# Attention with beacon keys, then an MLP: the first batch's scores by pairs of heads, and its first MLP products in two parts

## The chip, the cores and the metric

The kernel runs on one core of a Trainium2 chip. The metric is the device time of one execution in microseconds. Three runs of the kernel before took 323.22, 322.51 and 323.13 us: median 323.13 us.

## The reference

Batch 8, heads 8, 576 tokens of 64 elements, 16 beacon keys ahead of the 576 keys. The attention's output is laid out as 4608 tokens of 512 elements and goes through an MLP with 2048 hidden columns.

```
k_all, v_all = concatenate([beacon, own], axis=2)          # 592 keys
scores = q @ k_all.T / 8 ; token t sees all beacons and keys 0..t
a = softmax(scores) ; attn = a @ v_all                     # 8 x 8 x 576 x 64
x = attn as [4608, 512]
h = x @ w_in ; g = h * sigmoid(1.702 h) ; out = g @ w_out  # 512 -> 2048 -> 512
```

## The kernel before, in words

**Sets.** Four heads of one batch are a *set*; there are 16 (sets 0 and 1 are batch 0, sets 2 and 3 batch 1, and so on). A head's 64 elements lie as 32 partitions times 2, so the four heads of a set fill 128 partitions. q and k of a set (`qn`, `kn`) are loaded by one DMA each (L417) and turned by VectorE into `qT` and `kT` (L473; the beacon keys by a small one, L466). The values of a batch come in six loads: the beacons' (L422) and five blocks of keys, called V0 to V4 here (L426, L433).

**Scores and exponentials.** A set's causal scores are 1664 columns of a head, cut into *chunks*. For each chunk TensorE multiplies kT by qT head by head, each head in its own 32 rows of the array (`e_qk`, L506), and ScalarE takes the exponential into `E` (`e_exp`, L517). For batch 0, columns 0 to 511 of a set belong to the first half of its tokens (288), the other 1152 columns to the second half, in three chunks of 384. Diagonal blocks are masked, on VectorE with a `keep` tile (L531) for the first half of sets 0 and 1, else on GpSimd (L538); the `keep` tiles are made on GpSimd (L333, L334).

**Banks.** Of the 8 PSUM banks, four hold the tile `s`, one chunk's scores of four heads. The other four (`u0` to `u3`) are a ring for all other products; a bank opens again when the last reader of what it held (norm, z1, gate, evacuation) is done. In this kernel chunks 1 and 2 do not go to `s` but take all four ring banks, one a head, with four exponentials of one head each (`RINGED`); chunk 0 is read in two exponentials (`SPLIT`).

**Values and norms.** For a set and a half of its tokens there are three products of E (`e_av`, L597), for batches 0 and 1: one with `ones` for the sums (called x=2), one each for the even and odd elements of V. VectorE turns the sums into reciprocals (`z1` L607; `z2` L613 and L618) and the norm (L631) writes the result to `xT`.

**MLP.** Tokens are taken in groups: 0 to 255, 256 to 511, then 512 each. Of group 0 a *first product* `m1.0.n` makes two blocks of 128 hidden columns in one ring bank: 8 matmuls (`e_m1`, L655), over four slices of d_model, of which the first two come from set 0 and the last two from set 1. Then tanh on ScalarE (L669), the gate on VectorE (L688, which frees the bank), the second product (L700). Later groups use another gelu and a Strassen-like scheme (L769, L856). `w_in` comes in eight loads (L439): columns 0-511, 512-1023, 1024-1535 and 1536-2047 (a, b, c, d here), each in two halves of d_model (0 and 1); `w_out` in four loads (L446).

**Order.** Nothing is scheduled by the hardware or a search at build time: `op()` declares operations, numbered in order of declaration, with an engine, what they need and which ring bank they take, and the table `ORDER` lists by these numbers the order of every engine. `Plan.run` only goes through these lists; the planner's durations decide which ring bank a tile takes and how warm-up matmuls fill TensorE's first 20 us (L1377). Loads are issued by GpSimd, at most eight in flight: GpSimd waits at the ninth until the one eight earlier has landed, and all behind it in its order waits too, masks included.

The order of the first operations, decoded from `ORDER` (qk = a chunk's scores, av S.x.h = product x of set S and half h, m1.G.n and m2.G.t = first and second MLP products, turn S = transposition; VectorE's casts and memsets left out):

```
PE   qk0 qk3 qk1 qk4 qk2 qk5 av0.2.0 av1.2.0 av1.1.0 qk6 av0.0.0 av0.2.1 av0.1.0 av1.0.0 qk7
     m1.0.0 m1.0.2 m1.0.4 m1.0.6 av0.0.1 av0.1.1 av1.2.1 av1.1.1 av1.0.1 m1.0.8 m1.0.10 m1.0.14
     m1.0.12 m1.1.0 qk8 m1.1.4 m1.1.2 m1.1.12 qk9 ...
DVE  turn0q turn0k turn1k turn1q mask0 mask0 mask1 mask1 mask0 mask1 z1.0 z2.0 z1.1 z2.1 norm0 norm0
     norm1 norm1 z1.0 turn2q z2.0 gate gate gate norm0 norm0 z1.1 z2.1 norm1 gate norm1 gate turn2k ...
POOL q0 k0 k1 q1 V0 b1 a0 V4 a1 beaconV V2 V1 c1 keep b0 mask0 q2 k3 V3 c0 mask0 k2 d0 mask0 d1 mask1 q3 ...
```

(In this kernel qk0, 2, 3 and 4 are set 0's chunks in the order first half, then the three of 384; qk1, 5, 6 and 7 are set 1's.)

Of the kernel before, what the change touches and what calls it, by code (L numbers as in the profile page):

```python
# [8 lines left out]
F32 = mybir.dt.float32  # L9
AFT = mybir.ActivationFunctionType  # L10
# [51 lines left out]
    ],  # L62
    "DVE": [
# [23 lines left out]
    "POOL": [  # L87
# [8 lines left out]
    ],  # L96
# [6 lines left out]
    ],  # L103
# [4 lines left out]
    ],  # L108
}


# [133 lines left out]
def kernel(  # L245
# [13 lines left out]
    B, H, S, D = q.shape  # L259
# [1154 lines left out]
```

## Time and profile before

| what | value |
|---|---|
| median of three runs | 323.13 us |
| the profiled execution itself | 323.13 us |
| its span in the trace | 321.4 us, 10238 instructions |
| TensorE busy | 310.9 us, 97% |
| VectorE, ScalarE, GpSimd busy | 245.7, 219.9, 112.7 us |
| granted TensorE clock, 0 to 300 us | 1.00 |
| loads and stores, mean | 90 GB/s over the span |

The profile shares the span into 40 slices of 8 us and gives each engine's busy share in each in tenths, and the mean busy share of the DMA engines. The chain of waits follows the end of the program back through whatever released each piece of work. The timeline lists an engine's instructions in order, merged where alike: start, length, line, tiles, shape, count, and in brackets the idle time ahead of them with what ended it. Busy time of matmuls overlaps, so the start of the next entry tells how long one occupies TensorE, not its length.

### The profile page before, as it was taken

Reading aid. Unit: us, or ns where it says so; the run is one execution under the profiler, and the core shown is the slowest. Engines: PE = TensorE matmul, PEld = TensorE weight load, DVE = VectorE, ACT = ScalarE, POOL = GpSimd, SP = SyncE. Lnnn points to the kernel's source line nnn. Section 1 sums busy time; section 2 is a strip of 40 time slices with the busy share of each in tenths; the row PEclk is TensorE's granted clock in tenths of the full one; section 3 lists DMA queues with packets and bytes.
Section 4 is the critical chain, followed back from the end, with each engine's and each line's share of the span. In section 5 each row is a group of like instructions: output and inputs, shape, how many; then the busy total and the mean of one; then the engine's idle time right before and its main releaser. Section 6 shows DMA issues by size and latency. Waiting matters only on the chain.

```text
span 321.4 us, 10238 instructions
## 1 busy us (share of the span) xinstructions
PE 310.9 (97%) x4465; PEld 230.0 (72%) x4465; DVE 245.7 (76%) x481; ACT 219.9 (68%) x277; POOL 112.7 (35%) x178
## 2 busy tenths in 40 slices
PE   7779999999999999999999999999999999999995
PEld 6557765644886467754778878746888888888884
DVE  3579963997894888976888969888988975684683
ACT  1783778686767787598867685778779786665520
POOL 7777558590226703573083208320320000000000
PEclk9999999999999999999999999999999999999999
DMA  7999999998028961299174707700021000010113
GB/s 120 159 194 206 195 198 179 197 188 104 2 63 115 168 91 35 20 163 122 23 78 88 120 4 71 107 33 2 4 72 61 2 20 17 33 68 34 68 58 107
DMA packets 58222, 28.85 MB, mean 90 GB/s; under 512 B 41280, under 2 KB 53568, under 8 KB 58176
## 3 DMA queue, kind: packets, MB, share of 16 engines
q0 software_dynamic: 47552, 18.49, 49.4%
q1 hardware_dynamic: 10560, 9.69, 9.2%
q8 instruction: 35, 0.57, 0.7%
q14 instruction: 11, 0.09, 0.1%
q10 hardware_dynamic: 64, 0.01, 0.0%
HBM read 37.22 MB, written 9.44 MB: 145 GB/s over the span
## 4 chain that ended last, share of the span: by engine, by line
PE 91%; DMA 3%; POOL 3%; ACT 1%; issue 1%; DVE 0%; POOLq 0%
PE u L769 31%; PE u L655 26%; PE u L856 11%; PE u L597 10%; PE s L506 8%; PE u L700 5%; DMA w<-in_moe_w_in_dram 3%; POOL w L439 1%; ACT E L517 1%; POOL vb L433 1%; POOL kn L417 0%; ACT L676 0%; POOL qn L417 0%; POOL E L538 0%; DVE xT L631 0%
## 5 line engine op out<-in xcount | busy, mean ns | idle before, releaser
L517 ACT ACTIVATE E<-s 128x2048 f16<-128x2048 f32 (+5 forms) x63 | 95.6, 1532 | 41.4 <-PE s L506 37.7
L655 PE MATMUL u<-xT,w 128*128 128x256 f16 (+1 forms) x512 | 87.4, 326 | 0.7 <-issue 0.5
L538 POOL TENSOR_SCALAR_AFFINE_SELECT E<-E 128x512 f16<-128x512 f16 (+3 forms) x78 | 48.1, 634 | 91.4 <-ACT E L517 91.3
L655 PEld LDWEIGHTS <-w 128*128 128x128 f16 x512 | 49.3, 98 | 33.7 <-issue 2.1
L676 ACT ACTIVATE g<-u 128x512 f16<-128x512 f32 x80 | 43.4, 600 | 15.7 <-PE u L655 15.2
L769 PEld LDWEIGHTS <-g 128*128 128x128 f16 x512 | 48.4, 98 | 6.9
L785 DVE SCALAR_TENSOR_TENSOR osb<-u,osb 128x512 f32<-128x512 f32 x48 | 32.9, 685 | 22.8 <-PE u L769 18.2
L769 PE MATMUL u<-w,g 128*128 128x256 f16 x384 | 50.2, 273 | 0.0
L769 PEld LDWEIGHTS <-sA 128*128 128x128 f16 x384 | 36.6, 98 | 4.9
L506 PEld LDWEIGHTS <-kT 32*128 32x128 f16 x1376 | 24.6, 92 | 19.7 <-issue 12.8
L884 ACT ACTIVATE g<-u 128x512 f16<-128x512 f32 x48 | 27.0, 602 | 15.0 <-PE u L856 9.1
L506 PE MATMUL s<-qT,kT 32*128 32x32 f16 (+20 forms) x1328 | 33.1, 228 | 2.4 <-ACT E L517 1.9
L769 PE MATMUL u<-tB,sA 128*128 128x256 f16 x256 | 34.2, 273 | 0.0
L631 DVE TENSOR_TENSOR xT<-u,rz 128x352 f16<-128x352 f32 (+2 forms) x52 | 26.1, 519 | 6.1 <-PE u L597 5.3
L433 POOL DMA_DIRECT2D vb<-in_v_dram x32 | 27.5, 861 | 3.8 <-DMA qn<-in_q_dram 1.5
L597 PE MATMUL u<-E,vb 128*32 128x352 f16 (+8 forms) x928 | 27.3, 262 | 0.7 <-DMA vb<-in_v_dram 0.4
L597 PEld LDWEIGHTS <-vb 128*32 128x32 f16 (+1 forms) x928 | 20.0, 96 | 6.1 <-issue 2.1
L556 DVE TENSOR_TENSOR zs<-zs,E 128x1344 f16<-128x1344 f16 (+2 forms) x36 | 21.6, 601 | 1.1
L473 DVE STREAM_TRANSPOSE qT<-qn 128x576 f32<-128x576 f32 x16 | 19.8, 1235 | 3.2 <-DMA qn<-in_q_dram 2.4
L473 DVE STREAM_TRANSPOSE kT<-kn 128x576 f32<-128x576 f32 x16 | 20.1, 1257 | 0.9 <-DMA kn<-in_k_dram 0.3
L856 PEld LDWEIGHTS <-w 128*128 128x128 f16 x192 | 18.7, 98 | 2.2
L856 PE MATMUL u<-xT,w 128*128 128x256 f16 x144 | 20.1, 273 | 0.0
(76 smaller groups left out, 388.2 us busy)
## 6 DMA issues: line engine op xcount, KB each, us to landing
out_dram<-osb SPq DMA_DIRECT2D x36, 256.0 KB, 2.3
qn<-in_q_dram POOLq DMA_DIRECT2D x16, 288.0 KB, 6.4
kn<-in_k_dram POOLq DMA_DIRECT2D x16, 288.0 KB, 6.2
vb<-in_v_dram POOLq DMA_DIRECT2D x24, 128.0 KB, 5.5
w<-in_moe_w_in_dram POOLq DMA_DIRECT2D x8, 256.0 KB, 9.4
w<-in_moe_w_out_dram POOLq DMA_DIRECT2D x4, 512.0 KB, 11.1
vb<-in_v_dram POOLq DMA_DIRECT2D x8, 112.0 KB, 5.9
vb<-in_v_dram POOLq DMA_DIRECT2D x8, 80.0 KB, 6.6
```

The source lines that it names most:

```text
L433: nc.gpsimd.dma_start(out=t[0 : hi - lo, j, h0:h1, :], in_=v[b, h0:h1, lo:hi, :].rearrange("h n d -> n h d"),)
L473: nc.vector.transpose(out=f32(dst.rearrange("p n e -> p (n e)")).rearrange("p (r t) -> p t r", t=TR), in_=f32(src[:, :]).rearrange("p (t c ...
L506: nc.tensor.matmul(ss[i][h][:, o : o + w], kT[s % NB2][r : r + 32, j * P : (j + 1) * P, d], qT[s % NB2][r : r + 32, a : a + w, d], start=( ...
L517: nc.scalar.activation(out=Es[s][:, :, c0:c1] if h is None else Es[s][:, h, c0:c1], in_=sall[i][:, :, o : o + c1 - c0] if h is None else s ...
L538: nc.gpsimd.affine_select(out=blk, in_=blk, compare_op=ALU.is_ge, fill=0.0, base=off + (Nb if j == 0 else 0), pattern=[[0, Q], [1, w]], ch ...
L597: nc.tensor.matmul(u[32 * h : 32 * h + 32, a:e], lhs, src[0:kw, h, col : col + e - a], start=first, stop=last, skip_group_check=s >= EARLY ...
L655: nc.tensor.matmul(u[:, o + a - t0 : o + e - t0], w1t[:, kp, nt * P : (nt + 1) * P], xT[:, kp, a % XR : (e - 1) % XR + 1], start=(kp == 0) ...
L676: nc.scalar.activation(out=gts[g][:, n0:n1, 0:w], in_=rings[("m1", g, n0)][:, 0 : n * w].rearrange("p (n w) -> p n w", n=n), func=AFT.Gelu ...
L769: nc.tensor.matmul(u[:, HM * mt : HM * (mt + 1)], lhs[:, n, mt * P : (mt + 1) * P], rhs[:, n, :], start=(n == 0 and mt == 0 and p not in ( ...
L785: nc.vector.scalar_tensor_tensor(out=osbs[(g, dst)][:, :], in0=rings[("p", g, p)][:, :], scalar=scale_of(g), in1=osbs[(g, src)][:, :], op0 ...
L856: nc.tensor.matmul(u[:, HM * n : HM * (n + 1)], lhs[x][:, (2 * i + n) * P : (2 * i + n + 1) * P], rhs[:, x, :], start=fresh and n == 0 and ...
L884: nc.scalar.activation(out=gts[g][:, n : n + 2, HM * h : HM * (h + 1)], in_=rings[src][:, :].rearrange("p (n w) -> p n w", n=2), func=AFT. ...
```

## The change

Batch 0's chunks 0 to 5 get score tiles of their own in place of the ring: two tiles `p0` and `p1` of two banks, for heads 0 and 1 and for heads 2 and 3, which lie where `s` lies later. Chunk 0 ("F") has its scores in one go and two exponentials, one a pair; chunks 1 to 5 ("S") have scores and exponentials by pair, and a pair's scores wait only for the same pair's exponential of the chunk before. Chunks 6 and 7 use `s` as before. The chunks of batch 0 come in another order (set 0 first half; set 0; set 1 first half; set 0, set 1, set 0, set 1, set 1), and the first is not split by columns any more. The first products `m1.0.0` and `m1.0.2` are declared in two parts of two slices of d_model, each needing only one set's norms and one half of W1. `ORDER` is new for all engines; decoded in the same way:

```
PE   qk0 qk1 qk1 qk2 qk2 av0.2.0 av0.0.0 qk3 qk3 av0.1.0 qk4 av1.2.0 qk4 av1.0.0 av1.1.0 qk5 qk5
     m1.0.0(first) m1.0.0(second) m1.0.2(first) qk6 m1.0.6 av0.2.1 qk7 m1.0.4 m1.0.2(second) qk8
     av0.1.1 av0.0.1 av1.2.1 m1.0.8 qk9 m1.0.10 m1.0.12 qk10 av1.0.1 av1.1.1 m1.0.14 qk11 m1.1.0 ...
DVE  turn0q turn0k turn1q turn1k mask0 mask0 mask0 z1.0 z2.0 mask1 mask1 mask1 norm0 norm0 z1.1 z2.1
     norm1 norm1 gate turn2q z1.0 turn2k z2.0 gate gate norm0 z1.1 z2.1 gate norm0 gate gate ...
POOL q0 k0 beaconV q1 k1 V1 V2 V0 V3 b1 a1 a0 keep b0 q2 V4 k2 c1 mask0 c0 d1 d0 q3 mask0 mask0 mask1 k3 ...
```

From about the 95th operation of TensorE, the 47th of ScalarE, the 88th of VectorE and the 79th of GpSimd on, the order is that of before; SyncE's is unchanged.

```diff
+    EARLY1 = (0, 2)
-    SPLIT = True
...
-        CHUNKS += [[(s, 0, HF), (s, HF, EHALF)] if SPLIT and s < 1 else [(s, 0, EHALF)]] + [[(s, EHALF + cut * i, EHALF + cut * (i + 1))] for i in range(3)]
-    CHUNKS[: 4 * HS] = sorted(CHUNKS[: 4 * HS], key=lambda ch: ch[0][1] > 0)
+        CHUNKS += [[(s, 0, EHALF)]] + [[(s, EHALF + cut * i, EHALF + cut * (i + 1))] for i in range(3)]
+    CHUNKS[: 4 * HS] = [CHUNKS[x] for x in (0, 1, 4, 2, 5, 3, 6, 7)]
...
-    RINGED = (1, 2)
+    PAIRED = "FSSSSS"
...
-    def e_qk(i):
-        if i in RINGED:
-            ss[i] = [ring_tile(("qk", i, h)) for h in range(Q)]
+    def e_qk(i, p):
+        heads = {}
+        if i < len(PAIRED):
+            for p in range(2) if p is None else (p,):
+                sc = upper_pool("psp").tile([P, 2, 512], F32, tag=f"p{p}", name=f"p{p}")
+                sall[(i, p)] = sc
+                heads.update({2 * p + x: sc[:, x, :] for x in range(2)})
...
-                for h in range(Q):
+                for h, u in heads.items():
...
+        h0, h1 = (0, Q) if p is None else (2 * p, 2 * p + 2)
         nc.scalar.activation(
+            out=Es[s][:, h0:h1, c0:c1], in_=sall[(i, p)][:, :, o : o + c1 - c0], func=AFT.Exp, scale=0.125,
         )
...
-    def e_m1(g, n0, n1):
+    def e_m1(g, n0, n1, k0=0, k1=NKT):
...
-                for kp in range(NKT if a < e else 0):
+                for kp in range(k0, k1 if a < e else k0):
...
-                        start=(kp == 0),
+                        start=(kp == 0 and (k1 == NKT or nt == n0)) and k0 == 0,
                         stop=(kp == NKT - 1),
+                        skip_group_check=k1 - k0 < NKT,
...
+        halved = i < len(PAIRED)
+        split = halved and PAIRED[i] == "S"
+        for p in range(2) if halved else (None,):
+            if p is None or p == 0 or split:
+                y = p if split else None
+                before = [x for (j, n, z), x in exps.items() if j == i - 1 and y in (None, z)]
+                qks[i] = op(
+                    "PE", w, deps + before + ([qks[i]] if p else []), lambda y=y: e_qk(i, y), kind="qk", pr=0,
...
+            if g == 0 and n0 in EARLY1:
+                plan.partial.add(key)
+                pe, k = None, NKT // HS
+                for hs in range(HS):
+                    pe = op(
+                        "PE", k * n * (w / 2.4 + 2.8),
+                        [norms[(hs, 0, x)] for x in range(2)] + [w1_of[n0][hs], pe],
+                        lambda n0=n0, n1=n1, hs=hs: e_m1(g, n0, n1, k * hs, k * hs + k),
```

More of the change, by code (lines that the diff above doesn't have):

```diff
@@ L162, in run @@
         free = {e: 0 for e in todo}
-        free.update(POOL=900, SP=700)
+        free.update(POOL=1300, SP=700)
         mode, table, order = "m", "e", []
@@ L490, in qk_pieces @@
         return got
-    def e_qk(i):
-        if i in RINGED:
-            ss[i] = [ring_tile(("qk", i, h)) for h in range(Q)]
+    def e_qk(i, p):
[5 more added lines that the diff above has]
+                heads.update({2 * p + x: sc[:, x, :] for x in range(2)})
         else:
             sc = upper_pool(f"pss{plan.late_of(i)}").tile([P, Q, 512], F32, tag="s", name="s")
-            ss[i] = [sc[:, h, :] for h in range(Q)]
-            sall[i] = sc
+            sall[(i, p)] = sc
+            heads = {h: sc[:, h, :] for h in range(Q)}
         for (s, c0, c1) in CHUNKS[i]:
@@ L503, in e_qk @@
             for d in range(2):
-                for h in range(Q):
+                for h, u in heads.items():
                     r = 32 * h
                     nc.tensor.matmul(
-                        ss[i][h][:, o : o + w],
+                        u[:, o : o + w],
                         kT[s % NB2][r : r + 32, j * P : (j + 1) * P, d],
@@ L512, in e_qk, with e_exp @@
                     )
-    def e_exp(i, n, h=None):
+    def e_exp(i, n, p):
         s, c0, c1 = CHUNKS[i][n]
         o = sum(x[2] - x[1] for x in CHUNKS[i][:n])
+        h0, h1 = (0, Q) if p is None else (2 * p, 2 * p + 2)
         nc.scalar.activation(
-            out=Es[s][:, :, c0:c1] if h is None else Es[s][:, h, c0:c1],
-            in_=sall[i][:, :, o : o + c1 - c0] if h is None else ss[i][h][:, o : o + c1 - c0],
-            func=AFT.Exp,
-            scale=0.125,
+            out=Es[s][:, h0:h1, c0:c1], in_=sall[(i, p)][:, :, o : o + c1 - c0], func=AFT.Exp, scale=0.125,
         )
@@ L964, in chunk @@
             deps += [turn[(s, 0)], turn[(s, 1)]]
-        if i in RINGED:
-            key = [("qk", i, h) for h in range(Q)]
-            plan.partial.update(key)
-            for x in key[1:]:
-                deps.append(op("PE", 0, list(deps), lambda: None, pr=0, ring=x, mode="r", name=f"open{i}"))
-        elif i:
-            k = max(x for x in range(i) if x not in RINGED)
-            deps += [x for (j, n), x in exps.items() if j == k]
-        ps = [x[0] for x in qk_pieces(i)]
-        w = sum(2 * x / 2.4 + 10.5 for x in ps)
@@ L975, in chunk @@
-        qks[i] = op(
-            "PE", w, deps, lambda: e_qk(i), kind="qk", pr=0,
-            due=0, mode="r", name=f"qk{i}", ring=key[0] if i in RINGED else None,
-        )
-        for n, (s, c0, c1) in enumerate(CHUNKS[i]):
-            if i in RINGED:
-                for h in range(Q):
-                    x = exps[(i, h)] = op(
-                        "ACT", 65 + 0.8345 * (c1 - c0), [qks[i]], lambda n=n, h=h: e_exp(i, n, h), pr=0, name=f"exp{s}.{i}",
-                        table="e", closes=key[h],
-                    )
-                    parts.setdefault(s, []).append((c0, c1, x))
-            else:
-                x = exps[(i, n)] = op(
-                    "ACT", 65 + 0.8345 * 4 * (c1 - c0), [qks[i]], lambda n=n: e_exp(i, n), pr=0, name=f"exp{s}.{i}",
-                    table="e",
+        w = sum(2 * x[0] / 2.4 + 10.5 for x in qk_pieces(i))
@@ new lines, in chunk @@
+        halved = i < len(PAIRED)
[6 more added lines that the diff above has]
+                    "PE", w, deps + before + ([qks[i]] if p else []), lambda y=y: e_qk(i, y), kind="qk", pr=0,
+                    due=0, mode="r", name=f"qk{i}",
+                )
+            for n, (s, c0, c1) in enumerate(CHUNKS[i]):
+                x = exps[(i, n, p)] = op(
+                    "ACT", 65 + 0.8345 * (2 if halved else Q) * (c1 - c0), [qks[i]], lambda n=n, p=p: e_exp(i, n, p),
+                    pr=0, name=f"exp{s}.{i}", table="e",
@@ L991, in chunk @@
                 )
                 parts.setdefault(s, []).append((c0, c1, x))
+        for s, c0, c1 in CHUNKS[i]:
             for m, (j, a, e) in enumerate(MASKS if s < EARLY else WMASKS):
@@ L1295, in mlp @@
                 plan.partial.add(key)
-            pe = op(
-                "PE", 4 * n * (w / 2.4 + 2.8), xs + w1_of[n0] + old, lambda n0=n0, n1=n1: e_m1(g, n0, n1),
-                kind="m1", pr=g, ring=key, mode="m", name=f"m1.{g}.{n0}",
-            )
+            if g == 0 and n0 in EARLY1:
[6 more added lines that the diff above has]
+                        lambda n0=n0, n1=n1, hs=hs: e_m1(g, n0, n1, k * hs, k * hs + k),
+                        kind="m1", pr=g, ring=key, mode="m", name=f"m1.{g}.{n0}",
+                    )
+            else:
+                pe = op(
+                    "PE", 4 * n * (w / 2.4 + 2.8), xs + w1_of[n0] + old, lambda n0=n0, n1=n1: e_m1(g, n0, n1),
+                    kind="m1", pr=g, ring=key, mode="m", name=f"m1.{g}.{n0}",
+                )
             m1s.setdefault(g, []).append(pe)
@@ L1341 @@
                 empty = op(
-                    "DVE", 60 * (s1 - s0), [exps[(0, 0)]],
+                    "DVE", 60 * (s1 - s0), [exps[(0, 0, 0)]],
                     lambda s0=s0, s1=s1: nc.vector.memset(bkf[:, s0:s1, :], 0.0), due=due, pr=1, name="bk",
@@ L1362 @@
     for ph, i in enumerate(plan.breaks):
-        plan.late.append([x for (j, n), x in exps.items() if j == i])
+        plan.late.append([x for (j, n, y), x in exps.items() if j == i])
         if i + 1 < len(CHUNKS):
```

111 rows, old and new, of the table ORDER are left out of this document.

## The prediction

> **What bounds the kernel now.** I read the page first (busy shares by slice, then the chain of waits), then the chain in order of time for the first 30 us, then TensorE's timeline there, then the landings of single loads.
>
> ```profile
> PE   7779999999999999999999999999999999999995
> DMA  7999999998028961299174707700021000010113
> ...
> PE 91%; DMA 3%; POOL 3%; ACT 1%; issue 1%; DVE 0%; POOLq 0%
> ```
>
> TensorE is full in every slice (8 us each) but the first three and the last, and 91% of the chain that ends last is TensorE. The chain's other 9% lie almost wholly in the first 25 us. So only one question decides: how far does this change move the moment from which TensorE works without a gap? The DMA row is full for nine slices: in the head, loads stand in line.
>
> ```profile
> 6.52 10.27 DMA w<-in_moe_w_in_dram
> ...
> 17.96 0.69 POOL w L439
> ...
> 19.65 0.69 POOL w L439
> 20.34 0.01 issue
> 20.35 0.66 POOL E L538
> 21.00 0.04 issue
> 21.05 0.57 PE u L597 x19
> 21.62 0.02 issue
> 21.64 0.04 DVE xT L631
> 21.68 0.34 issue
> 22.02 0.82 DVE xT L631 x2
> 22.84 0.04 issue
> 22.88 1.80 PE u L655 x15
> 24.68 0.50 issue
> ```
>
> Columns: start, us, piece. The first MLP products (L655) run from 22.88, behind batch 0's norms (L631), behind value products (L597), behind a mask on GpSimd (L538) that stands in GpSimd's order behind weight loads.
>
> ```profile
> 11.63 0.54 PE L506 MATMUL s<-qT,kT 32*128 32x192 f16 x24
> 12.00 0.64 PE L506 MATMUL u<-qT,kT 32*128 32x288 f16 x24
> 13.74 0.55 PE L506 MATMUL s<-qT,kT 32*128 32x208 f16 x32 [1.11 <-ACT E L517]
> 17.04 0.54 PE L506 MATMUL s<-qT,kT 32*128 32x288 f16 x24 [0.81 <-ACT E L517]
> 17.51 0.71 PE L597 MATMUL u<-E,ones 128*32 128x288 f16 x24
> 19.43 0.54 PE L506 MATMUL s<-qT,kT 32*128 32x192 f16 x24
> 19.89 0.41 PE L597 MATMUL u<-E,vb 128*32 128x288 f16 x12
> ```
>
> Scores (L506) wait for exponentials to empty their banks (1.11, 0.81 us), and the first value product stands behind them at 17.51.
>
> **Durations used**, all from this trace: a chunk's scores 0.47 us on TensorE; an E product of twelve matmuls 0.25, of twenty 0.50; an MLP product of eight 0.92; exponentials 0.48 to the next at 512 columns and 1.35 at 1536, so 0.85 ns a column, 0.92 at 1024, 0.70 at 768, and 0.10 more to the result; VectorE: transposition 1.26, masks 0.2 to 0.42, z1 0.45, z2 0.73, norm 0.46, gate 0.68; GpSimd: mask 0.65 or 0.49, issue 0.55 to 0.9.
>
> **Loads.** Landings in the trace come in order of issue, one at a time. Their differences are each load's cost: k0 1.47, beacon V 0.18, q1 1.38, k1 1.49, V1 0.62, V2 1.57, V0 0.73, V3 0.52, V4 0.52; W1 (a, b: columns 0-511, 512-1023; 0, 1: half of d_model) b1 1.85, a0 1.97, a1 1.32, b0 1.29; q2 1.49, k2 1.45. A load is issued when the one eight earlier has landed (k0 lands at 7.52, the tenth issue starts at 7.80). The new order adds up to: q0 6.04, k0 7.52, beacon V 7.70, q1 9.09, k1 10.58, V1 11.2, V2 12.8, V0 13.5, V3 14.0, b1 15.9, a1 17.2, **a0 19.16** (14.94 before), b0 20.4, q2 21.9, V4 22.5, **k2 23.91** (28.21 before). Check: the first twelve are before's first twelve with V3 for V4, and before's twelfth landed at 19.16.
>
> **The change, step by step.**
> 1. Scores and exponentials. The first scores start at 8.93 as now. Exponentials of set 0's first chunk end at 9.64 + 2 x 0.92 = 11.5, of the second at 12.9; set 1's keys (k1 10.58) are transposed by 12.2, after q1's, so its scores start at about 12.3 and its exponentials end at 14.7; the next three chunks take 6 x 0.70, to 19.0. Banks empty by pairs, so ScalarE waits for nothing. Before, seven chunks were through at 21.49; now six at 19.0: no loss, and no gain by itself.
> 2. Masks and norms. GpSimd makes the keep masks behind the issue of a0 (q1's landing 9.09 + 0.28 + 0.7), so at about 10.1 to 11.3 (13.43 before), so set 0's masks end at 13.0, its first E products run at 13.4, z2 is done at 15.0, set 1's masks (behind it on VectorE) at 15.8, set 0's norms 16.7, set 1's z2 17.9, its norms **18.7** (22.83 before).
> 3. First MLP product. Both its parts need W1 of columns 0-511. Its first part needs a0, which lands at 19.16, later than every norm. So the start is 19.2, and the split brings nothing there: what the norms gain beyond that is lost to the later load.
> 4. To the next load. First product 0.92, first half of the second 0.46, scores 6 0.47, the fourth 0.92: to 21.95. Then set 0's second-half sum waits for two masks; GpSimd has the issue of q3 ahead of them, which waits for b0 (20.44 + 0.28), so 20.72 + 0.55 + 0.65 + 0.49 = 22.4. Then 0.50 + 0.47 + 0.92 + 0.46: 24.75.
> 5. Batch 1's scores (chunk 8) come next, at 34.05 before. They need k2: 23.91, transposition 1.26 and 0.14 around it: **25.31**.
> 6. From there both kernels run the same work in another order. Before, from chunk 8 to the start of chunk 18 (60.96) there are 26.91 us. The new order also has to do there what before had done by then: five value products (26.81 to 29.41, 2.60) and five MLP products (29.41 to 34.05, 4.64). New waits: the second product keeps its bank open until its gate, which stands on VectorE behind k2's transposition and z2 (26.47), so two value products wait 0.14 and 0.09, and later starts 0.23 together. 25.31 + 26.91 + 2.60 + 4.64 + 0.46 = 59.92, against 60.96: **1.04 us sooner**. From chunk 18 on the order of all engines is nearly the same, TensorE is full, and the loads behind (last W2 slice by the same sum 51.0, read at about 51.8) are just in time; the gain stands, or W2 eats some.
>
> The eight chunks of batch 0 take fourteen exponentials, before fifteen; that is in step 1. Half a chunk's scores uses two row groups, not four: 12 matmuls for 384 columns cost between 0.24 (half of 0.47) and 0.47 (no saving); I took 0.36. Both ends hide behind the other pair's exponential (0.70), and if they didn't, the 1.3 us of waiting for a0 would take them.
>
> More changes between scores, value and MLP products: 37 runs of one kind up to chunk 17, against 28. In the rows 24 scores followed by scores take 0.37 (11.63 to 12.00), followed by value products 0.46 (19.43 to 19.89): 0.1 a change. Four of the nine lie before the first MLP product, where TensorE waits for a0; between it and chunk 8 the waits for masks and k2 absorb them; from chunk 8 to 18 there are 21, and before 19 and two in the pieces I added. So 0. The Trainium skill (TensorEngine Tiling, Key Properties) says that changing the tiling mode, not just the tile, drains TensorE. The rows agree that it costs something, and at nine times 0.1 in the open the sum would be 0.9 us, nearly the gain.
>
> The profiled execution took 323.13 us, 1.73 around the span of 321.4, and is also the median of the three. So 323.13 - 1.04 = **322.1 us**.
>
> **Rivals.**
> - *Loads come sooner.* The two W1 loads at 1.85 and 1.97 cost 1.3 like the six others: a0 and k2 land 1.2 sooner, the first product starts at 18.8, chunk 8 at 24.1: 320.9. For it: both slow ones share one stretch of thin DMA rows (under 150 GB/s around 10 us). Against: that stretch has values in it, and the new order has more. Chance 0.2.
> - *The banks replace the wait.* Three of four ring banks are freed by gates that VectorE holds behind k2's transposition. If those come another 0.5 to 1 us late, or W2 does, TensorE pays it one for one: 322.6 to 323.1. For it: VectorE is busy from 21.9 to 30 in this order; the unexplained 0.50 before 25.18 may come too. Against: TensorE has a lead of under 0.2 only twice. 0.2.
> - *Slower: four value loads in a row each cost what V2 did.* 4 x 1.57 = 6.28 in place of 3.44 pushes a0, the masks' release and k2 by 2.8: 324.9. It decides from 1.7 us of lateness on. For it: small packets. Against: V1 behind V2 took 0.62, V3 0.52. 0.1. The Trainium skill (DMA: Bandwidth & Descriptors, Specifications) wants at least 512 B for line rate, with a read-modify-write below; 41280 of the page's 58222 packets are under that. Here q1 writes its 288 KB in 1.4 us, V2 its 128 KB in 1.57, V1 as many in 0.62: the trace agrees for one of them.
> - *The change doesn't do what it says:* the split part of it, in step 3, gains nothing and holds a bank; that is in the forecast. Forecast: 0.5, its own range 321.4 to 322.5.
>
> **Numbers.** A measurement of this kernel can tell about 0.2% (0.65 us) from no change: faster means under 322.5. Forecast and sooner loads make 0.7 faster; the banks 0.2 the same; the value loads 0.1 slower. Range 320.8 to 323.2.
>
> **What would show it.** Right: a0 landing near 19.2 and the first L655 right behind it; norms of set 1 done by 19; k2 near 23.9 and chunk 8 about 1.4 behind; no idle ScalarE between 9.6 and 19. Wrong: scores waiting over 0.6 us for L517 again; MLP products waiting for VectorE after 25 us by more than 0.5 in sum; a0 after 20; clock below 1.0 in the first 25 us.

## The result and the profile after

The changed kernel takes 325.15 us (median of 7 runs, 324.43 to 325.51), the kernel before 323.23 us (median of 7 taken beside them, 322.51 to 324.06). The ratio is 1.0054, with a 95% interval of 1.0038 to 1.0070: about 1.9 us **slower**, where 1.0 us faster had been forecast. The profiled execution took 325.41 us, its span is 323.7 us.

From the page of the changed kernel: busy tenths of TensorE and the DMA engines in 40 slices, the queue that carries instructions, and the chain of waits by engine.

```profile
PE   7998999899999999999999999999999999999995
DMA  7999999999016981289274806810011001010113
...
q8 instruction: 35, 0.57, 0.7%
...
PE 95%; ACT 2%; issue 1%; DVE 1%; DVEq 0%; ACTq 0%
```

The difference is small, but clear of its interval. TensorE now starts its full load sooner, but the fourth and the eighth slice (24 to 32 and 57 to 65 us) show 8, where the kernel before had 9. Its timeline shows what is missing there (start, length, line, tiles, shape, count, idle time ahead and what ended it), with the same places of the kernel before behind it:

```profile
19.56 1.54 PE L656 MATMUL u<-xT,w 128*128 128x256 f16 x12
...
23.21 0.53 PE L509 MATMUL s<-qT,kT 32*128 32x208 f16 x28
24.85 0.20 PE L509 MATMUL s<-qT,kT 32*128 32x32 f16 x4 [1.11 <-issue]
24.98 1.48 PE L656 MATMUL u<-xT,w 128*128 128x256 f16 x12
26.60 0.64 PE L509 MATMUL s<-qT,kT 32*128 32x288 f16 x24
...
31.05 0.20 PE L509 MATMUL s<-qT,kT 32*128 32x32 f16 x4 [0.48 <-issue]
...
36.97 1.48 PE L656 MATMUL u<-xT,w 128*128 128x256 f16 x12 [0.30 <-issue]
...
62.08 0.66 PE L509 MATMUL s<-qT,kT 32*128 32x336 f16 x24
...
64.41 2.30 PE L598 MATMUL u<-E,vb 128*32 128x288 f16 x88 [0.72 <-issue]
71.16 11.40 PE L656 MATMUL u<-xT,w 128*128 128x512 f16 x52 [0.31 <-issue]
```

The kernel before:

```profile
22.21 2.47 PE L655 MATMUL u<-xT,w 128*128 128x256 f16 x18
25.18 1.70 PE L655 MATMUL u<-xT,w 128*128 128x256 f16 x14 [0.50 <-issue]
...
34.05 0.64 PE L506 MATMUL s<-qT,kT 32*128 32x288 f16 x24
...
60.96 0.65 PE L506 MATMUL s<-qT,kT 32*128 32x336 f16 x24
```

The first MLP product (L656) starts at 19.56. In the kernel before its first matmuls ran at 22.21, 2.65 us later, and the rest without a wait from 22.88, the number that the chain of waits gives. But five gaps ended by "issue", by nothing that the profile shows, add up to 2.92 us. The first stands inside one chunk's scores: 28 of 32 matmuls run, nothing happens for 1.11 us, then the last four run. Nothing in the program separates them. The kernel before has one such gap (0.50, ahead of 25.18).

**Where the time went.**

| start of | before | forecast | after |
|---|---|---|---|
| first MLP product | 22.21 (the rest 22.88) | 19.2 | 19.56 |
| chunk 8's scores | 34.05 | 25.31 | 26.60 |
| chunk 18's scores | 60.96 | 59.92 | 62.08 |
| from there to the end of the span | 260.4 | 260.4 | 261.6 |

Chunk 18 is 2.16 late against the forecast; 1.11 + 0.48 + 0.30 = 1.89 of it are gaps. Behind it 1.2 are lost; 0.72 + 0.31 = 1.03 of that are gaps.

**What the gaps share.** In the record of TensorE's matmuls they stand ahead of the 352nd, 480th, 608th, 992nd and 1120th, all 96 + 128 k. The one of the kernel before also stands ahead of its 352nd, which is another matmul of another operation. The page has the key: queue 8 carried 35 packets of kind "instruction" with 0.57 MB, so 16 KB each; TensorE executes 4467 matmuls and as many weight loads, 8934 instructions, and 8934 / 35 is about 255. So a packet is a block of 256 instructions, 128 matmuls. The trace has each packet's times; here with the matmul that begins the block it brings ("behind": from the start of the block ahead of it to the packet's own start):

```
               block begins  packet     matmul  behind  gap
before         #352          22.89-23.78  25.18   3.46   0.50
before         #480          28.72-29.61  31.10   3.54   none
after          #352          22.58-23.51  24.85   3.93   1.11
after          #480          28.62-29.55  31.05   3.76   0.48
after          #608          34.76-35.74  36.97   3.71   0.30
after          #992          61.81-63.02  64.41   4.05   0.72
after          #1120         68.65-69.53  71.16   4.24   0.31
after, 85 to 100 us, little DMA: three packets      -1.3 to 1.0   none
```

In the rows where loads stand in line, a packet starts to move 3.5 to 4.2 us after the block ahead began, takes 0.9 to 1.2, and 1.2 to 1.6 us later its first matmul runs: the blocks with a gap came about 6 us behind the last (24.85 to 31.05 is 6.20, 31.05 to 36.97 is 5.92). The new order runs batch 1's scores, 24 to 32 small matmuls a chunk, from 26 us on instead of 34, and so needs the blocks faster than they come.

The views list no idle time under 0.15 us, so a short wait of this kind stays hidden. The changed kernel has one ahead of its 224th matmul, 96 + 128 again, in the value products ahead of chunk 5's scores: it starts at 18.66, 0.28 behind the 223rd and 1.28 behind the end of its packet (17.37).

**The theories.** *Code*: the gaps are waits for these packets. *Banks*: they are waits for PSUM banks behind VectorE that the profile doesn't name (a rival of the prediction). *Pairs*: the scores by pairs, or the split product, cost the time themselves.

### The profile page after: what moved, and what is told of

Read it like the earlier page. It is cut to its first block, busy times and chain, and to the rows that moved or that the text cites. A ratio compares the mean times of both kernels' runs of the same rounds, so it can differ in the third digit from the quotient of the medians.

```text
span 323.7 us, 10242 instructions
## 1 busy us (share of the span) xinstructions
PE 314.4 (97%) x4467; PEld 232.2 (72%) x4467; DVE 244.7 (76%) x481; ACT 220.0 (68%) x276; POOL 113.1 (35%) x178
## 4 chain that ended last, share of the span: by engine, by line
PE 95%; ACT 2%; issue 1%; DVE 1%; DVEq 0%; ACTq 0%
PE u L771 31%; PE u L656 25%; PE u L858 11%; PE u L598 10%; PE s L509 8%; PE u L702 4%; PE u L1380 3%; PE p L509 2%; ACT E L521 1%; ACT L678 0%; DVE osb L787 0%; ACT g L678 0%; DVE tB L327 0%; DVE zt L608 0%; DVE rz L619 0%
## 5 line engine op out<-in xcount | busy, mean ns | idle before, releaser
L521 ACT ACTIVATE E<-s 128x2048 f16<-128x2048 f32 (+3 forms) x58 | 89.3, 1553 | 37.7 <-PE s L509 34.0
L656 PE MATMUL u<-xT,w 128*128 128x256 f16 (+1 forms) x512 | 87.7, 326 | 0.7 <-issue 0.6
L656 PEld LDWEIGHTS <-w 128*128 128x128 f16 x512 | 49.1, 98 | 33.7 <-issue 2.0
L509 PEld LDWEIGHTS <-kT 32*128 32x128 f16 x1376 | 26.7, 92 | 19.3 <-issue 12.7
L509 PE MATMUL s<-qT,kT 32*128 32x32 f16 (+14 forms) x1224 | 31.2, 229 | 1.8 <-issue 1.6
L858 PEld LDWEIGHTS <-w 128*128 128x128 f16 x192 | 18.7, 98 | 2.2
```

Source lines behind the costliest of these rows:

```text
L509: nc.tensor.matmul(u[:, o : o + w], kT[s % NB2][r : r + 32, j * P : (j + 1) * P, d], qT[s % NB2][r : r + 32, a : a + w, d], start=(d == 0) ...
L521: nc.scalar.activation(out=Es[s][:, h0:h1, c0:c1], in_=sall[(i, p)][:, :, o : o + c1 - c0], func=AFT.Exp, scale=0.125,)
L656: nc.tensor.matmul(u[:, o + a - t0 : o + e - t0], w1t[:, kp, nt * P : (nt + 1) * P], xT[:, kp, a % XR : (e - 1) % XR + 1], start=(kp == 0 ...
L858: nc.tensor.matmul(u[:, HM * n : HM * (n + 1)], lhs[x][:, (2 * i + n) * P : (2 * i + n + 1) * P], rhs[:, x, :], start=fresh and n == 0 and ...
```

## The experiments

Medians; ratios against runs of the kernel before taken beside each group of four; chunk 18 from the profiled execution. "Further on" counts matmuls.

| kernel | us (range) | ratio, 95% | chunk 18 |
|---|---|---|---|
| e1 changed, whole last pieces | 325.39 (323.52 to 327.10) | 1.0057, 1.0035 to 1.0079 | 59.79 |
| e2 before, whole last pieces | 323.98 (323.05 to 327.10) | 1.0022, 0.9996 to 1.0047 | 62.09 |
| e3 changed, 20 further on | 329.02 (328.75 to 329.68) | 1.0176, 1.0156 to 1.0197 | 61.98 |
| e4 changed, no pairs | 328.77 (328.22 to 329.72) | 1.0167, 1.0145 to 1.0189 | 65.05 |
| e5 as e1, 54 further on | 321.23 (320.75 to 321.84) | 0.9927, 0.9905 to 0.9948 | 59.73 |
| e6 before, 20 further on | 326.60 (323.78 to 327.42) | 1.0070, 1.0038 to 1.0102 | 64.11 |
| e7 changed, 90 further on | 323.82 (323.49 to 325.08) | 1.0014, 0.9999 to 1.0030 | 61.05 |
| e8 as e1, 98 further on | 321.92 (320.46 to 322.65) | 0.9937, 0.9913 to 0.9961 | 60.04 |
| e9 as e2, 92 further on | 322.76 (322.46 to 323.50) | 0.9993, 0.9981 to 1.0004 | 60.80 |
| e10 as e5, dose at 31 us | 333.30 (332.82 to 333.55) | 1.0310, 1.0290 to 1.0330 | 71.49 |
| e11 as e5, dose at 122 us | 328.26 (327.83 to 329.47) | 1.0162, 1.0138 to 1.0185 | 59.27 |
| e12 as e5, first products whole | 321.42 (321.00 to 322.10) | 0.9945, 0.9928 to 0.9961 | 59.11 |

### Moving the blocks without touching the work (e3, e6)

The edit adds small matmuls to the warm-up, whose results nobody reads, in place of a few of its own. The work behind is the same, instruction by instruction; only its place in the program moves. This is the edit of e6; e3 has the same in other words.

```diff
+    few, cut = (24, 2) if until == FIRST else (0, 0)
-    for x in [f32(scrap)] * (n // 4) + [scrap] * (n % 4):
+    for x in [f32(scrap)] * (n // 4 - cut) + [scrap] * (n % 4):
         nc.tensor.matmul(idle[:, 0:COLS], x[:, 0:P], x[:, 0:COLS], start=True, stop=True)
+    for _ in range(few):
+        nc.tensor.matmul(idle[:, 0:32], scrap[:, 0:P], scrap[:, 0:32], start=True, stop=True)
```

> The changed kernel, with 24 matmuls of 32 columns in place of 2 of the 10 warm-up matmuls ahead of the first scores: nothing else moves, but every later instruction lies about 40 places (20 matmuls) further on in the program. Code theory: the gaps move to other matmuls by 20: in chunk 7's scores the gap comes after 8 of 32 instead of after 28, the next at the first matmul of chunk 9's scores instead of after 20 of 24, the third inside chunk 11's scores (after 16 of 32) instead of in the first product behind them; each 128 still cost 6.1 us, so the work behind the third gap is up to 20/128 x 6.1 = 0.95 us later: 325.2 to 326.2. Bank and pairs theories: gaps stay at the same matmuls (28 + 4, 20 + 4, 4 + 12), time within 0.2 us of the changed kernel's.

TensorE's timeline of e3:

```profile
23.32 0.36 PE L509 MATMUL s<-qT,kT 32*128 32x208 f16 x8
24.38 0.36 PE L509 MATMUL s<-qT,kT 32*128 32x96 f16 x24 [0.70 <-issue]
...
30.30 0.54 PE L509 MATMUL s<-qT,kT 32*128 32x288 f16 x24 [0.48 <-issue]
...
36.23 0.27 PE L509 MATMUL s<-qT,kT 32*128 32x48 f16 x16 [0.59 <-issue]
...
69.51 0.20 PE L509 MATMUL s<-qT,kT 32*128 32x48 f16 x4 [3.26 <-issue]
```

The gaps moved exactly as the code theory said: after 8 of 32, ahead of all 24, after 16 of 32; in the record they are again ahead of the 352nd, 480th and 608th (and one of 0.41 ahead of the 224th). In the changed kernel the last four matmuls behind the gap are the second half (d = 1) of a sum whose first half is already in the same banks, so no bank was waited for there; and a wait for banks has no reason to move by just these 20 matmuls when only the warm-up changes. That settles the banks theory. The size was not as expected: chunk 18 came no later (61.98), and the 3.9 us come from a block that nobody had counted, the 3.26 ahead of the 1120th matmul, and from the clock behind it (below).

> The kernel before, with 24 matmuls of 32 columns in place of 2 of the 10 warm-up matmuls (the edit of e3): every later instruction lies 20 matmuls further on. Code theory: counted out on the kernel before's own matmul starts, blocks that begin 20 matmuls sooner wait 1.9 us at about 22 us (where it waited 0.50 at 25) and 3.0 us at about 67 us, where it did not wait, with a clock drop behind it as in e3: 327 to 329. Every other theory: 323.2 within 0.3, since not one instruction of the computation is changed or moved.

e6's timeline:

```profile
21.79 0.54 PE L506 MATMUL s<-qT,kT 32*128 32x208 f16 x30
24.64 0.19 PE L506 MATMUL s<-qT,kT 32*128 32x32 f16 x2 [2.32 <-issue]
```

The kernel before, too, gets 3.3 us slower by a shift of 20 matmuls (326.60 against 323.29 beside it; two of its eight executions took only 323.78 and 324.38). The gap at 24.64 is the expected one (2.32 for 1.9), and chunk 8 starts at 37.20 for 34.05; the 3.0 expected near 67 us was only 0.24. So the kernel before owed part of its time to where its blocks happened to begin.

### Fewer matmuls for the same products (e1, e2)

```diff
-        if w > 64:
+        if w > 512:
             got[-1:] = [(w - 32, s, j, a, o), (32, s, j, a + w - 32, o + w - 32)]
```

> The changed kernel, with the last piece of a chunk's scores no longer cut into one of w - 32 and one of 32 columns: 8 matmuls fewer in each of the 36 chunks (4165 instead of 4453), the same products. Code theory (TensorE's own instructions come over DMA queue 8 in packets of 16 KB, 256 instructions or 128 matmuls with their weight loads; a packet waits behind the loads, so 128 matmuls can't take less than about 6.1 us in the head; the gaps 'issue' of 1.11, 0.48 and 0.30 us are this): fewer matmuls per us of work, so these three gaps shrink to under 0.4 us in sum up to 40 us, chunk 8 starts at 25.3 to 25.6 (26.60 now) and chunk 18 at 59.5 to 60.5 (62.08 now); a new wait for a packet behind the w_out loads around 60 to 65 us may give 1 to 2 us back: 322.5 to 324.5 in all. Bank theory (the gaps are waits for banks behind VectorE) and pairs theory (the pairs themselves cost the time): the gaps stay, chunk 18 and the end move by under 0.3 us (325.0 to 325.4).

The packets fell from 35 to 32. The three gaps between 20 and 40 us went; one of 0.71 stands ahead of 19.75, and 0.29 ahead of chunk 8's scores waits for the transposition of k2. Chunk 18 started at 59.79, 2.3 us sooner than in the changed kernel and 0.13 from the forecast. Then this, in e1's timeline:

```profile
63.44 0.61 PE L509 MATMUL s<-qT,kT 32*128 32x384 f16 x18
66.71 0.26 PE L509 MATMUL s<-qT,kT 32*128 32x48 f16 x6 [2.66 <-issue]
```

and in e1's busy times by window (us; busy of PE, PEld, DVE, ACT, POOL; granted clock, DMA share, GB/s):

```profile
66.00:70.00 4.00, 3.29 (x14) 1.30 (x15) 2.99 (x3) 2.97 (x4) 1.43 (x3) 0.50 0.89 99
70.00:74.00 4.00, 4.00 (x14) 1.51 (x13) 3.97 (x5) 1.93 (x3) 1.71 (x2) 0.66 1.38 178
```

A new wait of 2.66, more than the 1 to 2 us expected; and TensorE then worked at half its clock for 6 us (66.7 to 72.7), which nobody had expected. The profiled execution is the slowest of the eleven (327.10): the nine over 325 had a granted clock of 0.989 to 0.995 over the span, the other two 0.998 and 0.999, and these took 323.52 and 323.54, inside the expected 322.5 to 324.5. The median alone, 325.39, would have spoken for the rivals (325.0 to 325.4); chunk 18 speaks against them. The Trainium skill (TensorE: Matmul & The Clock Gate, HAM oscillation — how this bites in real kernels) asks for no idle gaps over about 3.4 us; here pauses of 2.32 (e6), 2.66 and 3.26 (e3) came with a granted clock of 0.50, one of 2.44 (e4) did not.

> The kernel before with the same edit (8 matmuls fewer in each chunk). Code theory: its one gap of 0.50 at 25.18 goes, chunk 18 starts 0.1 to 0.5 sooner (60.96 now); in the dense scores behind chunk 18 a wait for a packet of up to 2 us may appear; 322.5 to 325. Bank and pairs theories: within 0.3 us of 323.2, the 0.50 stays.

e2 can't be read as a test of the small gap: in its profiled execution the granted clock was 0.86 between 20 and 40 us (0.50 from 20 to 24, with no pause over 1.1 us in the 9 us ahead of its fall), so that chunk 18 came later, at 62.09. What lowered it there is open. Its 0.81 at 67.20, ahead of the 992nd matmul, is the new wait expected there. e9 is the clean form.

### Both together (e5, e8, e7, e9)

The waits at a given shift can be counted out on a trace's matmul starts, with 6.1 us from block to block. Shifts with almost none were taken.

> The kernel of the whole last pieces (e1), with 60 matmuls of 32 columns in place of 3 of the 10 warm-up matmuls: every later instruction lies 54 matmuls further on in the program. Code theory: in e1 one block of 128 matmuls lay just over the dense scores and values between 60.6 and 64.1 us and had to wait 2.66 us; moved by 54 it is shared between two blocks. Counted out on e1's own matmul starts with 6.1 us from one block to the next: gaps of 0.1 to 0.3 at about 23, 29 and 62 us, 0.6 in sum, so the 2.66 goes, and the half clock behind it: chunk 18 at 59.6 to 60.2, the end 1.0 to 1.5 sooner than the kernel before: 321.7 to 322.4. Bank theory, or a wait for the w_out loads: the gap of 2.66 stays at the same scores, 325.4.

e5's timeline around batch 1's first scores:

```profile
22.83 1.49 PE L656 MATMUL u<-xT,w 128*128 128x256 f16 x12
25.64 0.64 PE L509 MATMUL s<-qT,kT 32*128 32x288 f16 x24 [1.33 <-DVE rc L614]
```

No gap ended by "issue" is left in e5's first 90 us. What chunk 8 waits for is now what the prediction named: k2, landing at 24.23 here, and its transposition, which ends at 25.58 (the profile names a reciprocal that VectorE runs across it). Chunk 18 starts at 59.73:

```profile
59.73 0.65 PE L509 MATMUL s<-qT,kT 32*128 32x336 f16 x24
```

At 321.23 us this kernel beats the kernel before and the changed one.

> As e5, with 108 matmuls of 32 columns in place of 5 warm-up matmuls: 98 further on. Code theory: one wait of 0.4 at about 27 us and none later: chunk 18 at 59.4 to 60.0, 321.6 to 322.3; against e5 within 0.4.

> The changed kernel, with 100 matmuls of 32 columns in place of 5 of the 10 warm-up matmuls: every later instruction lies 90 matmuls further on. Code theory, counted out in the same way: 1.3 to 1.7 us of waits at about 20 us, 0.1 at 27, 0.4 at 33, none at 64 and 71: 1.8 us in place of 2.9, so 1.0 us faster than the changed kernel: 323.6 to 324.6. Bank and pairs theories: 325.2, the gaps at the same matmuls.

Both times came out in their ranges, 321.92 and 323.82. e8 shows no gap ended by "issue" in the first 90 us, not even the 0.4 expected; still its chunk 18 starts at 60.04, just over the expected 60.0, and it is 0.69 slower than e5, not within 0.4. In e7 the waits for packets were 0.78 at 20.68, 0.36 at 32.80 and 0.72 at 64.38, 1.86 in sum for 1.8, but the first smaller than expected and the last where none was expected.

> The kernel before with the whole last pieces (e2) and 102 matmuls of 32 columns in place of 5 warm-up matmuls, 92 further on: by the count on e2's matmul starts no wait for a packet up to 75 us is left. So this is the old order freed of these waits, as e5 is the new one. Code theory and the prediction's own sum: the 0.50 of the kernel before goes, 322.4 to 323.2, and e5 stays 1.0 to 1.6 us faster: that is what the change itself is worth. If the change is worth nothing: within 0.4 of e5's 321.2.

322.76, in the range. Chunk 18 in its timeline:

```profile
60.80 0.66 PE L506 MATMUL s<-qT,kT 32*128 32x336 f16 x24
```

So with both orders freed of these waits the new one is 1.5 us faster in e5 (322.76 to 321.23) and 0.8 in e8, and the intervals of their ratios don't touch e9's. Chunk 18 starts 1.07 sooner in e5 and 0.76 in e8; the prediction had worked out 1.04.

### The same dose where loads queue and where they don't (e10, e11)

The edit of e10, in the kernel of e5; e11 has chunk 30 in place of 10.

```diff
+        w, s, j, a, o = qk_pieces(i)[0]
+        for x in range(64 if i == 10 else 0):
+            for h, u in heads.items():
+                nc.tensor.matmul(
+                    u[:, o : o + 32], kT[s % NB2][32 * h : 32 * h + 32, j * P : (j + 1) * P, 0],
+                    qT[s % NB2][32 * h : 32 * h + 32, a : a + 32, 0], start=True, stop=True,
+                )
```

> e5's kernel with 256 more score matmuls of 32 columns ahead of chunk 10's scores (31.2 us, loads in line), whose result the real scores overwrite; 256 is two blocks, so all later blocks begin at the same matmuls. Code theory: their own time, 7 to 8.4 us at 27 to 33 ns each, would need a new block every 3.5 to 4.2 us, but one comes each 6.1: chunk 12 starts 10.0 to 11.5 us later than in e5. Any theory without the packets: the same delay as in e11.

> The same 256 matmuls ahead of chunk 30's scores (122.3 us, where the DMA engines are 2% to 18% busy). Code theory: a packet asked for there starts within 1 us, so a block comes in 3.2 us or less and nothing waits: 6.9 to 8.5 us later, 2 to 4 us less than in e10, and no gap 'issue' of over 0.3.

TensorE's timeline of e10:

```profile
30.96 1.06 PE L508 MATMUL s<-qT,kT 32*128 32x32 f16 x112
34.25 1.19 PE L508 MATMUL s<-qT,kT 32*128 32x32 f16 x128 [2.23 <-issue]
40.44 0.29 PE L508 MATMUL s<-qT,kT 32*128 32x32 f16 x16 [5.01 <-issue]
40.57 0.80 PE L516 MATMUL s<-qT,kT 32*128 32x192 f16 x16
```

and of e11:

```profile
121.56 1.68 PE L508 MATMUL s<-qT,kT 32*128 32x32 f16 x187
125.77 0.73 PE L508 MATMUL s<-qT,kT 32*128 32x32 f16 x69 [2.53 <-issue]
126.32 1.04 PE L516 MATMUL s<-qT,kT 32*128 32x448 f16 x16
```

The matmuls took 9 ns each (1.06 us for 112), not the 27 to 33 I had put down, so the expectation for e11 was wrong in one point: it, too, had to wait. In e10 chunk 12 started 11.76 us later than in e5 (49.59 for 37.83), just over the expected 10.0 to 11.5. But the contrast is the one in question. The work behind the dose starts 9.61 us later in e10 (30.96 to 40.57), 4.76 later in e11 (121.56 to 126.32). A full block of 128 took 6.19 us in e10 (34.25 to 40.44), its packet starting 3.83 behind the block ahead; in e11 3.76 us (122.01 to 125.77), the packet starting 1.34 behind. This full block is what to compare: part of the 9.61 to 4.76 is that e11's first border, at 122.01, cost nothing, since the block ahead had begun 6.5 us before it. Half clock follows in both (0.50 from 40.4 to 46, 0.71 in the mean from 126.4 to 136). So the price of a matmul depends on the traffic: in the head this dense block cost 6.19 / 128 = 48 ns a matmul (the one ahead of it, 5.14 us, 40), at 122 us 3.76 / 128 = 29, though the matmuls are of the same length.

### Parts of the change (e4, e12)

```diff
-                before = [x for (j, n, z), x in exps.items() if j == i - 1 and y in (None, z)]
+                before = [x for (j, n, z), x in exps.items() if j == i - 1]
...
-                    "PE", w, deps + before + ([qks[i]] if p else []), lambda y=y: e_qk(i, y), kind="qk", pr=0,
+                    "PE", w, deps + before + ([qks[i]] if p else []), lambda y=y: e_qk(i, None) if y != 1 else None, kind="qk", pr=0,
```

> The changed kernel without the pairs: chunks 1 to 5 have the scores of all four heads together, which wait for both exponentials of the chunk before, in the same banks; order, split first product and load order as in the changed kernel; the same number of matmuls. Code theory: ScalarE waits 0.3 to 0.5 at each of five chunks, so the first MLP product starts up to 2 us later (19.56 now), but the gaps at 24.85 and 31.05 shrink by as much, and chunk 18 moves by under 0.7 us: 325.0 to 326.0. Pairs theory: 1 to 2 us faster than the changed kernel, 323.2 to 324.2. By the sum of the prediction alone: up to 2 us slower, 327.

Without pairs the first MLP product starts at 21.20 instead of 19.56: the pairs are worth 1.6 us there, and the pairs theory, which had forecast 323.2 to 324.2, falls at 328.77. The gaps at 24.85 and 31.05 shrank from 1.59 to 0.52 in sum, as expected. Not expected was the next one:

```profile
39.36 0.21 PE L509 MATMUL s<-qT,kT 32*128 32x32 f16 x5 [2.44 <-issue]
```

It stands ahead of the 608th matmul again; its packet started only 5.16 us behind the block ahead, the latest of all that TensorE waited for. Why that one took longer than 4.2 is open. With this gap and one of 1.06 at 72.02 the time is over all three expectations; chunk 18 came 2.97 later, not under 0.7.

```diff
-                        lambda n0=n0, n1=n1, hs=hs: e_m1(g, n0, n1, k * hs, k * hs + k),
+                        lambda n0=n0, n1=n1, hs=hs: e_m1(g, n0, n1) if hs == HS - 1 else None,
```

> e5's kernel with the first products m1.0.0 and m1.0.2 in one part each again (all eight matmuls where the second part stood). The prediction held that the split gains nothing: within 0.3 us of e5 (321.0 to 321.6). If the split is what makes the new order work: slower by the 0.46 us of half a product or more, 321.7 to 322.2.

321.42 for 321.23, with ranges that overlap: the split gains nothing that shows, as the prediction held. Chunk 18 even starts 0.62 sooner here, with k2 landing 0.62 sooner (23.61 for 24.23).

## Why the prediction was wrong

- **Step 1, scores and exponentials: right in kind.** ScalarE waited for scores by at most 0.45 at once. The last of the six chunks ended at 20.9 instead of 19.0: k1 landed at 11.20 (10.58 by the sum), and the gaps of 0.2 to 0.45 add up.
- **Step 2, norms: late by 1.3.** Set 1's norms end at 20.0 instead of 18.7 (19.2 in e5), with the exponentials ahead of them.
- **Step 3, first product: 19.56 for 19.2.** a0 landed at 18.62, sooner than the 19.16 forecast; TensorE was still at chunk 5's scores (18.80 to 19.56), so its own queue came last and not the load. These scores didn't wait for exponentials: the one they needed had ended at 18.13. The 224th matmul, with its hidden wait, stands right in front of them. The prediction also took 22.88, where the chain has the rest of it, for the start of the first product before; it was 22.21. The split indeed gains nothing (e12).
- **Loads: right in sum, in part by luck.** k2 landed at 23.46 for 23.91. The four value loads cost 0.74 to 0.90 each, so the slower rival (1.57 each) is refuted, though the result is on its side. The rival of sooner loads had its condition fulfilled (b1 1.24, a0 1.35 for 1.85 and 1.97), but k1 landed 0.62 late, so a0 and k2 came only 0.54 and 0.45 sooner, not 1.2. One trace doesn't settle this: e8 issues the same loads in the same order, and there b1 cost 2.40 and k2 landed at 24.54.
- **Steps 4 and 5, chunk 8 at 25.31: failed, 26.60.** In the changed kernel k2 was turned by 25.08, but 1.11 us of waiting for a packet, inside chunk 7's scores, held TensorE; step 4 has these scores at 0.47 and no such wait. Without it (e5) chunk 8 starts 1.4 behind k2's landing, just as the step said.
- **Step 6, chunk 18 at 59.92 and "the gain stands": this is the step that failed.** It took durations of pieces from the trace as if TensorE could issue them back to back in any order. From chunk 8 to 18 came 0.48 + 0.30 of packet waits, and 0.72 + 0.31 behind it. Freed of them, chunk 18 starts at 59.79 (e1) and 59.73 (e5), with 8 fewer matmuls in each chunk; the changed kernel's own 62.08 less its 1.89 of gaps is 60.19. So the rest of the sum was right to 0.3 us, in e5 by two errors that cancel: chunk 8 came 0.33 late (25.64), and the stretch from there took 34.09 for 34.61.
- **The rival "the banks replace the wait"** named the unexplained 0.50 ahead of 25.18 as something that "may come too". It did come, three times over before 40 us, but for another reason than banks. That line was in the chain, in a kernel whose page counts 35 instruction packets; explaining it instead of listing it would have given the slower rival, with its price: blocks 5.8 us apart, read off the two packets at 22.89 and 28.72 of the kernel before.
- **The signs of being wrong** that the prediction listed (scores waiting for L517, MLP products for VectorE, a0 after 20, a lower clock) did not show. All four watch the waits that it knew of; none watches the program's own arrival.

The Trainium skill (Runtime: NRT & Kernel Launch, Instruction fetch mechanics) does say that instructions are refilled in blocks of 16 KiB, 256 instructions, by a DMA queue of the sequencer's own while the block ahead runs, and that crossing a block is mostly hidden. This trace agrees on the block and disagrees on the hiding: 2.92 us in the changed kernel, up to 5.01 at once in e10. The prediction does not weigh it.

## What to carry to other kernels

An idle gap that is ended by "issue" has a cause: count the matmuls up to it in the record. Here the gaps lay a fixed number apart, whatever operation stood there, and the cause was the arrival of the program itself; the queue that carries instructions shows when each block came. Where loads keep the DMA engines full, look at how many matmuls an order puts into each 6 us, not only at how long they take: a shift of a few dozen instructions in idle time alone (e3, e6), or together with fewer, wider matmuls (e5), moved these kernels by 3 to 4 us with the same products. And compare two orders only after both are freed of such waits, else the place of the block borders is part of what is measured.

## What the runs showed of the hardware

- TensorE's program came in packets of 16 KB, 128 matmuls with their weight loads. With loads in line a block that TensorE waited for in the first 40 us came 5.1 to 6.4 us behind the last (7.6 once, e4); at 122 us, with the DMA engines 18% busy, 3.76.
- With a pause of TensorE of 2.3 to 5.0 us the granted clock fell to 0.50, for some 3 to 6 us behind it (e1, e3, e6, e10, e11), which by an estimate from these lengths cost 1.7 to 3.1 us more. With 2.44 in e4 it stayed at 1.00, and in e2 it fell with no pause over 1.1 us in the 9 us ahead, so what sets it is not settled here.
- A score matmul of 32 columns that uses a quarter of the rows took about 9 ns when 128 of them came in a row (1.19 us in e10).
